# The memory product of an Infini-attention kernel in sixty-four by thirty-two tiles, with a new order of the whole program

## The chip, the cores and the metric

The kernel runs on one core of a Trainium2 chip. The metric is the time of one execution on the device in microseconds; each version is run several times and its median counts. Beside the timed runs there is one profiled execution, whose trace gives start and length of every instruction. TensorE appears in it twice: PE is the matmuls, PEld the loads of their stationary operand ("weights"). DVE is VectorE, ACT is ScalarE, POOL is GpSimd, SP is SyncE, which issues most DMAs.

## The reference

A token sequence of 2048 rows of 512 goes through two branches, which a gate per row mixes. Branch A is attention with 32 heads of 16 in four segments of 512 rows; each segment attends causally within itself and reads a memory that the segments before have built. Branch B is a gated feed-forward net of width 1792. Cut to what matters here:

```
for s in range(4):
    p = softmax(qs @ ks^T * scale + causal mask)
    a_dot = p @ vs                                   # the value products
    pq = phi(qs)
    a_mem = (pq @ M) / (pq @ z + 1e-6)               # the memory is read
    outs.append(g * a_mem + (1 - g) * a_dot)
    pk = phi(ks)
    M = M + pk^T @ vs                                # the memory product
    z = z + sum of pk over the rows
a = concat(outs) @ wo
b = ((x@W_gate) * (x@W_gate > 0) * (x@W_up)) @ W_down
out = gate * a + (1 - gate) * b
```

M holds, for each head, a 16 x 16 matrix; z holds 16 numbers for each head.

## The kernel before, in words

**Layout.** Activations and weights are bf16 and stay in SBUF; sums are made in PSUM, which has eight banks of 128 partitions x 512 float32. Queries and keys are held transposed, in four groups G of 128 rows, a group being eight heads of 16. Values are held by tokens (`vaug`), 17 columns for each head: 16 values and one more that stands for a one, so that the product of weights and values gives the normalizer as its 17th column, and the memory product gives z as its 17th.

**Stages of a segment.** `proj` (line 546) makes q, k and v; `att` (line 650) the scores as 18 "quads" for each segment, into banks 0 to 3 together, one ScalarE exponential for each quad (line 666), the causal masks on GpSimd (line 670), and the value products (`fpv`, line 685, the matmuls in line 694). A half of the value products, for two of the four groups, is two calls of 64 matmuls each. They use 64x32 tiles of TensorE: the contraction is over 64 keys, the row half p picks partitions 0 to 63 or 64 to 127, and each of four column tiles takes the 17 columns of one head; row half 0 sums in one bank, row half 1 in another. Then `nd` (line 619) reads the memory (`num`, line 626, and three VectorE steps in lines 633 to 635), `ffn` (line 740) makes the feed-forward net's hidden layer, `outp` (line 764) its second half and the attention's output, and stores.

**The memory product.** `mu` (line 598) makes it after segments 0, 1 and 2. For each group G and each of four token tiles tt it issues two matmuls in 128x64 tiles (`mode="c"`, line 610): the contraction is over the 128 tokens of the tile, the stationary operand is 64 columns of phi(k), that is four heads, and the moving operand is the same four heads' 68 columns of `vaug`. That makes 4 x 4 x 2 = 32 matmuls, all in one PSUM bank. In each 64 x 68 result only the four diagonal blocks of 16 x 17 are wanted. One VectorE addition, `mum` (line 611), adds the whole 128 x 272 to `Mc`; four GpSimd products (line 615) spread it with a mask to the block diagonal form `Mbd16` that `num` reads, four heads' worth of columns twice.

**What sets the order.** Nothing is ordered by the loops. The program lists all operations with what they read and write, an estimate of how long each holds its engine, and for matmuls the tile mode: f is the full array, r the 32-row tiles of the quads, c the 128x64 tiles, h the 64x32 tiles. `Sched.run` (line 276) then places them in the order written out in the string `ORDER`: two characters stand for a number in base 62, half of it is the operation's number and its parity the engine, where two engines are possible. `BANKS` gives the PSUM bank of each new sum in turn. The order comes from a search outside of the kernel, which uses the same estimates; in `place` (line 220) a change of mode costs it 100 ns (`SWITCH`), and the memory product 520 ns. `place` also puts the waits on semaphores ahead of each operation. Each engine then runs its own list strictly in that order.

Line 705 makes the memory product wait for all that the first value products wait for; line 703 lists it ahead of them.

Of the kernel before, what the change touches and what calls it, by code (L numbers as in the profile page):

```python
# [26 lines left out]
ORDER = (
    "caambOaabQacbSbUaebWbYb8agb0aob2aiaqakcccecgciasckcmcocqcscYaucucwcyeKawfcfOggeMayfefQgicAcCaAcEcGcIcKaCeOcMfgcQcScOfSaEgkeQcUcWfifUbmgmeSbqeUeWeYfkfm"
    "foe1fqfWfYf0f2aGftgogqgsguaIe2f5aKe4gxbifufwe7g4bse8g6aMfagYaOfyg9g0aQf6aSg3hgbof8higygAaUm8gCaWhaaYgbhohcbkhqhsfEhenankfGhua0nwgca2nhnmnyntnogIncfIhI"
    "nqnFfMhKlinugSlkgKbegUfAbufChUa4lcgehWgWnea6legEmQnia8mSlgc0fKnUmVh2gMmeh4lmnWbgmgc2dilYbamKc8n2iegQmiial0ighkmMdclsgGgOlul2hAnImPhmiqlwnKiiishEhMlEnR"  # L30
    "iknMhOl4lAnYbGdglrl6deiClyn0bcl8hwlGb4dknOn4iEdqicoih6hGnSokhQnAbIlIhYmqiyoriOiunCb6lLbMc4omiwnGiQm2iGm4h0bKoolCn6oshSn8lOhCmsiKofdsiWh8oulplQoam6iSiY"
    "owhymumWiAociIoDmYimogi8dam1iUjkiMjajwiojmlSdujyjCmAjgjAjYi0wmjqj0wojcwsi4wqwujsjEoGwxjGkajIoIkcoKjOj2oMjejMwCi2wEi6oOkikeoyj6oQkkkgoAwGjoo4o6oEpskmku"
    "jQpcpEmckwlMoSjKkoo8j4padwoUpemkdypGjukGlUjio1pgkqkIpummpijSpNkCbwpIkylWpKppkAkSpOpkkKkUkEwObAjUoWbyoYjWkOpmkso2k4kMwQk0k6pBw8j8xak2pqkWpwwSkQpyxdkYpY"
    "pCqmk8p0ladAqoqqdCbCqsqaycqcquyeqwyiygykbEqyx6yqsOqCx8sQxAqExoqAxCxqqGybxUdEs0xtxWqIdGs2qKxex0qMx2xYxgdms8c6qOmwtamamoqQqSdomCqUmyxjtkmEqWx5qYxEmItgtm"
    "q0sWq2dIr6q8q4titcdKr8q6twqisaratetyscrssSsYsewAsgrusUsirwdMsktEmGtIsms4rcqetKyup6ymtodQqkywsoyotQtUysqgrytWsMtGreyDtArAsKp2sqtsrgssp8risuxKtut2swdUrk"
    "s6dSt4tYsArCtMsCrmsEp4rEsGtSrGwYuarouetquqtCrIrquguCtOust0rKucuEpQuIwIuGu8rMpSvauKwKySuMyUuOpUrOuWy0rQvgumyWxuuUsyvizsuiyYwMzupWyGy2uwrSuQzAvkyIvmw0yK"
    "yPzkyMw2zgyQvsvozivudWrUwWzQdYzpzSw6zmxnvAvEzqukzwvGuAsIrWwUzywyHyzZvcHAvezCvQvMrYHCvSvwr0vCHsd0HUr2d2Huw4v2xwHIHwv4z2uYHKxyHWz4u0HZuSyydOweAawazUu2HN"
    "yAd4wgIkyEd6ImwczWvqy4xIz0vUy8Ipvyy6xGzauozdzEt6A0zev6IwuuA2zGxMu4IyvIzIt8IAzKvKzMH4uyBcvYzOBowiBed8H6v0BuAev8BsvWAgH9A8DcAmIaBgDeDmDgA4eaIcxlegDowkDi"
    "z6Bir4AiIfvODqAkDsDUz8DWAoAOAQBwAcACAEByAWBqBAAKBCD6AGBID8JgBGAIIYxOAqBKxSEaJiAMBkEeAsEcEgI0AzxQAuAwBMu6I4AAJoEqDSI6I3HQeiISHHJdASAUEsBOIUAYIMekIGIWDQ"
    "IOEuBQECI8EwEEBSJaBEIIJeDuDYCeIQEKEOBaCgDkIKEQEyCiemBUeoBmCkEmE0EABWEGE2BYESB0EoB2D2DwEUCmD0DyE8DAEiB4DCFaD4CoEMDGEIB6DIE4CqDKE6CsDMHOA6B8EkCuDOFkEWFw"  # L40
    "FmCaFcFIEYFyCceqFKIqFOesFACwGeFMCyDEGgFQCSFSHSCAH2ecHEGqCUFUGsCWeuCCCEF2ewGmCGGiGyIsCIIuGACYFWFGCKFsCMF0GoC0FEGKF4C2COGuGMFCC4eyC6JkFgC8NYFeeAGWN0GSJQ"
    "N2GYFiJmN4FoJSGkJqJEFuJGFqJZeCG8GCN8JNG4HaJIGGJKOaGEOcJsGOOeJuGwHkGUJOJwHgHmF6J2JBHcJyG0JUGIJCJ4G6LMF8JWLOKbGQKeG2KgJ0HiJ6HoJ8KmHeLYKcLQMaL0HqGaLSMcLU"
    "MgMeOGL6OEKiL8OIMiKkL2KqMkKoKsMmKCKyKEMsOOKGKKL4KIMuH1OSKOMwOUGcKQKMLgLcMoLeKWLiLlK0O0LmKuO2MyKwMAK2K4KAKSIjMCO4PcOWKUK8MEK6KYPeLoLAMqLsLaLCIgLqIFFYPo"
    "ICN6LILELxPgLuPqO8eeSyOKLyDaLGOMOgSCLKOYSALWPASGPiMGeGPsPCCQPwOiOCOQMIOkPkSEOmPuMKOoPaPMO6MMSIPOPEOsPIMOeIOuPmMQOwPKMSOyPyMUPQPUMWQiPSPWPGQkQoQmQONkQQ"
    "QqQsS8QuTaNmQCQWNoQAP6M0P8M2M4M6TgNEM8Q8NaRaNqS0NcNeQ0NgNsQ2NGQENiSWOqSYS2S5RwMYNuS6RyNwTwNITySKTFRkSMRmNySTNKNMQGQwTARsTcNAQaRIP2TeRKQYSOTiQSSQRgTCRc"
    "NORATGRUQ4NQSURWReNSRoTIQITURCTKRQTMTRP4T6RqUaQKRuUmRSTkPYTmRYT8RMTtToQeUeTONUQgUiQcTSTqNWQ6TWOAP0TuUcRETYROUgUGRGNCT0QUT3UkRiR0UKUrUIUSUPUMUuT4UoUyUs"
    "UUU4UQUwQMUWUDUAU6UER2U1R4R8VdUYVUQyU8U2VgR6VWVYSaV0ScVASeViSkVaVCSmVEV2SoVGSqSgVkVmVeVIeEV4SsVKVoSuWeV6SiVqSwVsVuVMVwVOVyV8VRWgWaWiWkWmWcWoVSWqWsWyWA"
    "WCWEWvWGWIWKWMWwWOWQ"
)
# [284 lines left out]
def program(sc, nc, T, PS, A_x, A_wq, A_wk, A_wv, A_wo, A_beta, W_g, W_u, W_d, gate_w, out, NSEG, KT, NF, NT, EPS, SCALE):  # L334
# [260 lines left out]
    def va(s):  # L595
        return [f"va{s % 2}_{tt}" for tt in range(4)] + ["vone"]

    def mu(s):

        ep = Epoch()  # L600

        def fn(e):
            for G in range(4):
                for tt in range(4):
                    for j in range(2):
                        ins = e.matmul(A(ep)[64 * j:64 * j + 64, 68 * G:68 * G + 68], lhsT=V.phik[:, tt, 128 * G + 64 * j:128 * G + 64 * j + 64],  # L606
                                       rhs=V.vaug[:, s % 2, tt, 8 * G + 4 * j:8 * G + 4 * j + 4, :].rearrange("q h c -> q (h c)"),
                                       start=(tt == 0), stop=(tt == 3), tile_position=(0, 64 * j), skip_group_check=True)
# [2 lines left out]
        d = dve(lambda e: e.tensor_tensor(V.Mc[:], V.Mc[:], A(ep)[:, 0:272].rearrange("q (g c) -> q g c", g=4), ALU.add), t_dve(272), reads=["Mc"], writes=["Mc"], name=f"mum{s}", ep=ep, role="r")
# [294 lines left out]
```

## Time and profile before

| | us |
|---|---|
| median of 3 runs | 263.08 |
| the runs | 262.85 to 263.32 |
| profiled execution | 262.51 |
| its span (first to last instruction) | 261.1 |
| busy in it: PE, PEld, DVE, ACT, POOL | 258.0, 115.8, 186.9, 179.1, 105.9 |
| the memory product's matmuls (L606), 96 | 2.1 busy |
| its addition on DVE (L611), 3 | 0.44 each |
| its products on POOL (L615), 12 | 0.47 each |

The granted TensorE clock is 1.0, full speed. PE's ends are modelled from pipelined starts, so the starts and the chain of waits say more than its busy time. Lines such as L606 are lines of the kernel; "ps<-vaug,phik" names the tile written and the tiles read; "128*64" in a matmul's row is the tile of the array, rows by columns; "x32" is the count. In the timeline the first column is the start, the second the time from the first start to the last end of the group, and brackets tell how long the engine sat idle before it and what ended that. In the chain of waits the columns are start, time, engine, what, and count.

### The profile page before, as it was taken

How to read it: one execution, taken by the hardware profiler on the slowest of the kernel's cores; microseconds unless marked ns; L12 is line 12 of the kernel's file. 1: busy time of each engine (PE TensorE's matmuls, PEld its weight loads, DVE VectorE, ACT ScalarE, POOL GpSimd, SP SyncE). 2: the span in 40 equal slices, each digit the busy share in tenths (PEclk: the TensorE clock that was granted, in tenths of full speed). 3: DMA queues.
4: the chain of work that ended last, by engine and by line, in shares of the span. 5: the costliest groups of instructions: out<-in, count | busy, mean ns of one | idle time of the engine just before them, and what ended most of it. 6: DMA issues, size and time to landing. Idle time of an engine off the chain costs nothing.

```text
span 261.1 us, 6450 instructions
## 1 busy us (share of the span) xinstructions
PE 258.0 (99%) x2665; PEld 115.8 (44%) x2665; DVE 186.9 (72%) x370; ACT 179.1 (69%) x154; POOL 105.9 (41%) x283
## 2 busy tenths in 40 slices
PE   8999999999999999999999999999999999999997
PEld 4644435443544454434544353435344543445444
DVE  1269888698895488888878489778886516568951
ACT  3697988997887897785868687788887765500001
POOL 2010566658106943527511853775057001870000
DMA  6999952018502643220015222002023001020002
GB/s 197 261 247 212 216 86 45 4 41 233 169 25 59 135 99 62 63 62 0 23 29 122 63 60 63 3 0 46 3 55 72 3 20 41 3 60 0 3 3 80
DMA packets 34684, 19.34 MB, mean 74 GB/s; under 512 B 24032, under 2 KB 34144, under 8 KB 34656
## 3 DMA queue, kind: packets, MB, share of 16 engines
q1 hardware_dynamic: 34272, 18.67, 29.6%
q8 instruction: 21, 0.34, 0.5%
q10 hardware_dynamic: 384, 0.27, 0.3%
q14 instruction: 7, 0.06, 0.1%
HBM read 9.87 MB, written 2.11 MB: 46 GB/s over the span
## 4 chain that ended last, share of the span: by engine, by line
PE 97%; DMA 1%; ACT 1%; ACTq 0%; DVE 0%; issue 0%
PE ps L750 38%; PE ps L789 19%; PE ps L563 10%; PE ps L662 9%; PE ps L694 7%; PE ps L782 6%; PE ps L561 5%; DMA hT<-in_A_x_dram 1%; PE ps L626 1%; PE ps L554 1%; PE ps L606 1%; ACT L381 0%; PE ps L461 0%; ACTq L368 0%; DVE osb L798 0%; ACT rden L381 0%
## 5 line engine op out<-in xcount | busy, mean ns | idle before, releaser
L666 ACT ACTIVATE E<-ps 128x2048 bf16<-128x2048 f32 x72 | 135.1, 1877 | 38.0 <-PE ps L662 37.6
L670 POOL TENSOR_SCALAR_AFFINE_SELECT E<-E 128x256 bf16<-128x256 bf16 (+1 forms) x256 | 98.3, 414 | 123.2 <-ACT E L666 61.4
L750 PE MATMUL ps<-xT,wu 128*128 128x512 bf16 x224 | 60.8, 380 | 0.0
L750 PE MATMUL ps<-xT,wg 128*128 128x512 bf16 x224 | 60.0, 380 | 0.0
L789 PE MATMUL ps<-wd,hT 128*128 128x512 bf16 (+2 forms) x238 | 55.9, 367 | 0.0
L761 DVE TENSOR_TENSOR hT<-ps,rl 128x512 bf16<-128x512 f32 x56 | 38.2, 685 | 14.8 <-PE ps L750 13.1
L750 PEld LDWEIGHTS ps<-xT,wg 128*128 128x128 bf16 x224 | 20.7, 98 | 26.5 <-issue 2.4
L759 DVE TENSOR_SCALAR rl<-ps 128x512 bf16<-128x512 f32 x35 | 23.9, 686 | 11.0 <-PE ps L750 10.7
L750 PEld LDWEIGHTS ps<-xT,wu 128*128 128x128 bf16 x224 | 20.4, 98 | 25.7 <-issue 3.2
L789 PEld LDWEIGHTS ps<-wd,hT 128*128 128x128 bf16 x238 | 21.2, 98 | 24.0 <-issue 3.7
L662 PE MATMUL ps<-qT,kp 32*128 32x128 bf16 (+7 forms) x512 | 28.6, 287 | 0.0
L708 DVE STREAM_TRANSPOSE Tn<-ps 128x512 f32<-128x512 f32 x32 | 21.2, 696 | 3.8 <-PE ps L694 3.4
L798 DVE TENSOR_SCALAR osb<-ps,omg 128x512 bf16<-128x512 f32 (+1 forms) x15 | 10.6, 718 | 16.9 <-PE ps L789 9.9
L662 PEld LDWEIGHTS ps<-qT,kp 32*128 32x128 bf16 x512 | 8.2, 92 | 27.7 <-ACT E L666 12.3
L799 ACT ACTIVATE osb<-ps,omg 128x512 bf16<-128x512 f32 (+1 forms) x2 | 1.3, 634 | 26.8 <-PE ps L782 26.8
L563 PE MATMUL ps<-xT,wk 128*128 128x512 bf16 x64 | 17.9, 380 | 0.0
L694 PE MATMUL ps<-E,vaug 64*17 64x128 bf16 (+7 forms) x512 | 17.8, 283 | 0.0
L694 PE MATMUL ps<-E,vsh 64*17 64x128 bf16 (+7 forms) x512 | 17.6, 283 | 0.0
L561 PE MATMUL ps<-wv,xT 128*128 128x512 bf16 x64 | 17.3, 380 | 0.0
L758 ACT ACTIVATE rl<-ps 128x512 bf16<-128x512 f32 x21 | 12.4, 595 | 6.0 <-PE ps L750 4.6
L782 PE MATMUL ps<-wo,oT 128*128 128x512 bf16 (+2 forms) x68 | 16.3, 367 | 0.0
L694 PEld LDWEIGHTS ps<-E,vaug 64*17 64x17 bf16 x512 | 12.2, 86 | 3.6 <-issue 0.8
(71 smaller groups left out, 226.8 us busy)
## 6 DMA issues: line engine op xcount, KB each, us to landing
vsh<-vaug SPq DMA_DIRECT2D x8, 272.0 KB, 3.3
out_dram<-osb SPq DMA_DIRECT2D x15, 128.0 KB, 1.8
wg<-in_B_W_gate_dram SPq DMA_DIRECT2D x8, 224.0 KB, 3.2
wu<-in_B_W_up_dram SPq DMA_DIRECT2D x8, 224.0 KB, 4.0
osb<-in_A_x_dram SPq DMA_DIRECT2D x12, 128.0 KB, 2.0
wd<-in_B_W_down_dram SPq DMA_DIRECT2D x3, 512.0 KB, 6.4
wq<-in_A_wq_dram SPq DMA_DIRECT2D x4, 128.0 KB, 3.0
wk<-in_A_wk_dram SPq DMA_DIRECT2D x4, 128.0 KB, 3.3
```

The costliest lines, as they stand in the source:

```text
L561: ins = e.matmul(A(ep)[:, :], lhsT=V.xT[:, kt, s % NX, col * 128:(col + 1) * 128], rhs=w[:, kt, :], start=(kt == 0), stop=(kt == KT - 1))
L563: ins = e.matmul(A(ep)[:, :], lhsT=w[:, kt, col * 128:(col + 1) * 128], rhs=V.xT[:, kt, s % NX, :], start=(kt == 0), stop=(kt == KT - 1))
L662: ins = q.matmul(PS[:, jj, o:o + 512 - 64 * c], lhsT=V.kp[r, kslot(s, G), c, :], rhs=V.qT[r, qslot(s, G), 64 * c:512], start=True, stop=Tr ...
L666: acts.append(act(lambda a: a.activation(V.E[:, e, :, :], PS[:, 0:4, :], ACT.Exp, scale=SCALE), t_act(2048), writes=[f"E{e}"], name=f"exp{ ...
L670: pools.append(pool(lambda g, ap=ap, base=base: g.affine_select(out=ap, in_=ap, compare_op=ALU.is_ge, fill=0.0, base=base, pattern=[[0, 4] ...
L694: ins = q.matmul(A(eps[2 * g + p])[32 * jj:32 * jj + 17, 64 * c:512], lhsT=v[:, 8 * G + 2 * jj + p, :], rhs=V.E[r, e, jj, o:o + 512 - 64 * c],
L708: ds.append(dve(lambda e, p=p, ep=eps[2 * (G - G0) + p]: e.transpose(V.Tn[:, p, :], A(ep)[:, :]), 706, writes=[f"Tn{p}"], name=f"tr{s}_{G} ...
L750: ins = e.matmul(A(ep)[:, :], lhsT=w[:, kt, f * 128:(f + 1) * 128], rhs=V.xT[:, kt, c % NX, :], start=(kt == 0), stop=(kt == KT - 1))
L759: ("dve", lambda e, ep=eg, r=r: e.tensor_scalar(V.rl[:, r, :], A(ep)[:, :], 0.0, None, ALU.max), t_dve(512))],
L761: evs.append(dve(lambda e, ep=eu, r=r, hs=hs: e.tensor_tensor(V.hT[:, hs, :], A(ep)[:, :], V.rl[:, r, :], ALU.mult), t_dve(512), reads=[f" ...
L782: ins = e.matmul(A(ep)[:, 0:c1 - c0], lhsT=V.oT[:, o0 + G, i * 128:(i + 1) * 128], rhs=V.wo[:, G, c0:c1], start=st_ and G == 0, stop=sp_ a ...
L789: ins = e.matmul(A(ep)[:, 0:c1 - c0], lhsT=V.hT[:, slots[f], i * 128:(i + 1) * 128], rhs=V.wd[:, f, c0:c1], start=st_ and f == f0, stop=sp ...
```

## The change

The memory product is issued in the 64x32 tiles of the value products. For each group G and token tile tt there are eight matmuls: row half p (64 of the 128 tokens) by column tile j (32 columns of phi(k), two heads), with the two heads' 34 columns of `vaug` moving. That makes 4 x 4 x 2 x 4 = 128 matmuls. Row half 0 sums in one bank, row half 1 in another. `Mc` keeps 34 columns for each group where it kept 68; two VectorE additions of 128 x 136 add the two banks to it, one after the other. The four GpSimd products spread it to `Mbd16` as before, two heads' columns four times. The estimate for the product is 430 ns in mode h.

The estimate for the transposed loads of x (`load_x`) becomes 190,000 bytes and 1200 ns of SyncE where it was 131,072 and 1350, and the order and the banks are searched anew with these numbers. An unused constant goes. The diff without the strings:

```
-        ("Mc", [128, 4, 68], F32), ("Mbd16", [128, 4, 136], BF16), ("mumask", [128, 4, 136], F32),
+        ("Mc", [128, 4, 34], F32), ("Mbd16", [128, 4, 136], BF16), ("mumask", [128, 4, 136], F32),
...
-                           1 << 17, occ=1350.0, writes=[f"xT{c % NX}_{kt}"] + ([] if c % NX else [f"xT0_{kt}{h}" for h in range(2)]), name=f"ldx{c}_{kt}"))
+                           190000, occ=1200.0, writes=[f"xT{c % NX}_{kt}"] + ([] if c % NX else [f"xT0_{kt}{h}" for h in range(2)]), name=f"ldx{c}_{kt}"))
...
     def mu(s):
 
-        ep = Epoch()
+        eps = [Epoch(), Epoch()]
+        eps[0].group = eps[1].group = (eps[0], eps[1])
 
         def fn(e):
             for G in range(4):
                 for tt in range(4):
-                    for j in range(2):
-                        ins = e.matmul(A(ep)[64 * j:64 * j + 64, 68 * G:68 * G + 68], lhsT=V.phik[:, tt, 128 * G + 64 * j:128 * G + 64 * j + 64],
-                                       rhs=V.vaug[:, s % 2, tt, 8 * G + 4 * j:8 * G + 4 * j + 4, :].rearrange("q h c -> q (h c)"),
-                                       start=(tt == 0), stop=(tt == 3), tile_position=(0, 64 * j), skip_group_check=True)
+                    for p in range(2):
+                        r = slice(64 * p, 64 * p + 64)
+                        for j in range(4):
+                            ins = e.matmul(A(eps[p])[32 * j:32 * j + 32, 34 * G:34 * G + 34], lhsT=V.phik[r, tt, 128 * G + 32 * j:128 * G + 32 * j + 32],
+                                           rhs=V.vaug[r, s % 2, tt, 8 * G + 2 * j:8 * G + 2 * j + 2, :].rearrange("q h c -> q (h c)"),
+                                           start=(tt == 0), stop=(tt == 3), tile_position=(64 * p, 32 * j), skip_group_check=True)
             return ins
-        m = pe(fn, 520.0, reads=[f"phik{g}" for g in range(4)] + va(s), name=f"mu{s}", ep=ep, role="w", mode="c")
-        d = dve(lambda e: e.tensor_tensor(V.Mc[:], V.Mc[:], A(ep)[:, 0:272].rearrange("q (g c) -> q g c", g=4), ALU.add), t_dve(272), reads=["Mc"], writes=["Mc"], name=f"mum{s}", ep=ep, role="r")
+        m = pe(fn, 430.0, reads=[f"phik{g}" for g in range(4)] + va(s), writes=[eps[1].res], name=f"mu{s}", ep=eps[0], role="w", mode="h")
+        d = [dve(lambda e, p=p: e.tensor_tensor(V.Mc[:], V.Mc[:], A(eps[p])[:, 0:136].rearrange("q (g c) -> q g c", g=4), ALU.add), t_dve(136), reads=["Mc"], writes=["Mc"], name=f"mum{s}_{p}", ep=eps[p], role="r") for p in range(2)]
...
-            j2 = lambda t, G=G: t[:, G, :].rearrange("q (j c) -> q j c", c=68)
-            ps.append(pool(lambda e, G=G, j2=j2: e.tensor_tensor(j2(V.Mbd16), V.Mc[:, G, :].unsqueeze(1).to_broadcast([128, 2, 68]), j2(V.mumask), ALU.mult), t_pool(136, 2.2),
+            j4 = lambda t, G=G: t[:, G, :].rearrange("q (j c) -> q j c", c=34)
+            ps.append(pool(lambda e, G=G, j4=j4: e.tensor_tensor(j4(V.Mbd16), V.Mc[:, G, :].unsqueeze(1).to_broadcast([128, 4, 34]), j4(V.mumask), ALU.mult), t_pool(136, 2.2),
...
-                put(dmu=[mem[1]], poolmu=mem[2])
+                put(dmu=mem[1], poolmu=mem[2])
```

The strings `ORDER` and `BANKS` are replaced as a whole. In the new order the set of operations is the old one with three more additions. The three memory products stand where they stood, between a quad and the first value products. At the start, TensorE has the query products and the transposes of the first input more mixed, the two filler matmuls first, all four k products ahead of the first quad, and v behind it; in the middle the feed-forward and output products are distributed anew among the quads; the last value products come seven TensorE groups earlier. The choice between VectorE and ScalarE changes for some fifty PSUM copies and the like.

More of the change, by code (lines that the diff above doesn't have):

```diff
@@ L17 @@
 LAT = 60.0
-MU_G = 1
 PE_LAT = 175.0
@@ L27 @@
 ORDER = (
[L28 to L47, printed above, removed]
@@ L48 @@
-    "WCWEWvWGWIWKWMWwWOWQ"
+    "bYbObQcYamaaacaeagaoaqaicaciakauccckayascscecmcucqcgcocwggeKfObScyaweMfccAfeaYfQaKcEcGcCcKcScIgicQcMcOfSgkeOfgfifkfmaCeQeSbqaAcUfobUeUeWaEcWgmfqeYe0fs"
+    "gogqc0fUfWfYaGf0bWb4f2b6f5gsaIgue2e4bee6f6f8b0fufwgbbsb8e8fagwgygAhggcc2c8hagefzfAgDhcfGhegGgYg0hifCgSgUhsg2g4g6g8fEnanmhuc4aOaMbkncgWbininohInynvnAbo"
+    "bmmSlemUhwhKhAhCfIlggKhUgEaQmWaWlilklmgIhWaUc6nKhyhQhohSlulwh2nHaShknenglzmYa0lon8m0baoah4iagMdciem3ignMiiiknkmMnCimmOnEhYh0iqnTlGfMlIbuhmmRdihMhOdemg"
@@ new lines @@
+    "nIhqisiymiiAlLmsmudgbgmkdkiCiEiKgOiGl0l2ocoemwlAnqiOl4ohm4nsnOoim6hEnwlClEnWm8nYicl6lPioiQnQiun4nUiWa6a8lSoogQmml8man0dmoklqoma4a2owiYfKlQotn2oqn6ouoy"
+    "h6h8dqi8hGjkjmiIoEjojybIjEdoiSiUiwiMjAjCb2lsjabMbGjgj0dajwbKwqjcwsj2wujibcwwwywBwGjGdsjIjKj4kckej8jQwIoIoKjOjeo6o8kgj6wLoRkkkaoMoAoOoCjupii4kmkojMkqkw"
+    "oSjsmCpkkioGpfpakypckAoUduoWo2kskuprpukIdwdykCkEkKkQjSjUjWkSpGpglUpIkMkOjYpKpMi6pOpwpQmokUoYjqo0o4xci0i2kWk2bApDxexhkYwSk6pmlMpok8dApypsk0wUpAkGwXp0qo"
+    "lak4pEdClcqqmyp2p8qabCquqcqeygqsyiqwqylYykbyymyoyasQyuycdEqAqExsxubwx4x6sSsUxxs2s4yexExGqGxYx0xiqIx3taqCqKqMqObEsWxkqQqSqUqkqmtctetitkp4mftmtoqWqYtus6"
@@ new lines @@
+    "x9s8lWdGsOmAmcq0mqmEq2mGxIxmdImKq4dKdQtyq6r8sap6q8tAwDrarurwscsetKtMsgsisktwryrArCtOsmsorEqgqitSyytWyAyHyqysywtYt0rGrItgt4mIssrcsuswsysYrergsMrirLsCrk"
+    "sEsGsqsIrmt6rowMt2tQtqugrrs0usuuuwuGtGtstItCtEuitUuIuouKuMt8uOdSuQvcvew0uSuYdUyCyEvguauUrOrQyIdWvorsu0pUrSrUrWyOvqwOwQucyKvwxoyMrYr0xyyTvywEyWvkviuyu2"
+    "u4yYy4yQyUvIy8zczedYd0zazhy0uEzivKvUuew2vWy2y6vMr2u6zwzUr5ukumzyzFzWv6sKzAv8wazkw4sAu8w6vazmvYzozqzszCzuxOvEwipWuAvGpYvQvAvOxKxNzGvmwZpSH0H2v0z3zIzKHE"
+    "HyvSHAwkzRzMHGwezOH5A4d2d4uWIqHJA6vCHCz6Isuqz8xAvszSvuIvBsuCAexCBgAaxQxSdMAiBwBiIaIcIfAcd6AkAqDqByDgv2v4d8zYz0eaAgIgIiwgICxWrMIEDixrIlAmAoDkDsDmDuDwBc"
@@ new lines @@
+    "xUIHDYAGAIz4ASAUwmwoAswcBuBABCBEBKxaD0AOEaAKA0HOHQBoISBGBMBOBQDWr6DUAMEcEiD2D4IUHTIWAWAYEkEqecBSEmAuA2AwA8BaAQEuI4EeI6egAyADEwIMAAEGI9JaJeIOdOEIw8IRBq"
+    "AEJcekJgESEUBUEWBWEYBIEOEQD6D8JiEgBYCiB0emB2E0E4E6eiE8BeB4B6B8CaCcJkDKDMEsDAHUDyIYI0DCI3CkCmCoCqDOEyIwDQDEFcFeDoBkDGECEKEMEEeoJmCeeqCsCuCwCyJoJuFoeeEo"
+    "BmFAesFOE2FCFEFaEADIFUFIFGFqFsFuFQGkCCFMFSeuCWHWCEGmGsDSFWFYF0F6F2F8GwCGGyCICYCKC0GAGEGCGGGMGIFkHKCMCOFKeweyHYeAC2C4CQGoGQGSCAC6GUFwFyHMC8GYG0DaDdFmJq"
+    "IoIyCgCSIAGWGaGcN4G2GOG4HaN6DeJsJKJMN8OaJWJYGeJwJSHeHcJ5OeOgOiJyJOJQOkHgHiJAHqJ8JUFgKaJCJEJ0H8FiJHJIHkGKHsHuLSJ2J6KkLUKmKsHmHoHwKcKeL4KhKiGqGuMgL6GgMk"
@@ new lines @@
+    "G6G8MiMmMoOKOMKoOOKqKwKyKuKEMqMsMuKIKKL8OYOUOWKQMaMyKAMcMeKCKUO0O2H6MAKYK0KWOIO6KGInK3LiLkKMKOeCO8PaLuLwPiPkeEK4KSL0LaLcLCF4K6PeMCLrLmK8L2PmPuLfLoMwLg"
+    "LyS2LsLALGLILWPwMEPyPALEMGMIPCPECUPGLKPgLOSESGLMLYSQSSGiMKPIPqOcS4PSPKLQMMSNMOMQSZTbILIJPMO4MSeGeIPsPoMUMWOQOSPUPWPYMYM0P0M2PcQoQuPOPQQqP2P4P6M4QUP8M6"
+    "M8NaNcQWQYQaQsQcNeQwQeNgNiQyQAQIQ2SINkQkQmReRgNKQ4SKSONMNmRiNORmRoRkQGQ6Q8NoNqNsTeNuRCNQNSTgRaQgNwRERGRKNyQ0RqRsRuRyTnRAOoNARwRINUNWNYOqNCOsOuROS6QKQM"
+    "QCQOS8TcN1RQSUSWTiS0R0TCTETkTLUYToU0R2UcOyOAOCQQOmOEOGUgOwTGTITMTONENGRMTQRWUeUlTSUiTUTqUmTsUsUoUqTXTYUxTzTuUuUyUMTwTAUORST4T0UQRUUST2T6UVRYU7QiRcT9Ua"
@@ L49 @@
+    "R8SeR4R6SaScQESgSiSkSqVGVmNIVoVqVsU2U4UEUAUCSsUWVIWkV0WmU8VaV2SuWoWqSmSwVeSySAV4V6VuSCUGVgVcVKVMN2SoV8WsUJUKVjVkVwVyQSVAVCVEVOVQVSVUVWVYWaWcWeWgWuWwWy"
+    "WiWEWGWIWKWMWOWAWCWQWSWUWW"
 )
 BANKS = (
-    "450674654756475765745645767654764674564765657467564465466754675454675674674544454657641757457547546754674567456134675764574656746574755645675456475476"
-    "5476456754546754675645746744457654674664465452604131675031742365310265"
+    "326454654754674656756456546574654764756476565745645675475464756747457464654667667465476546767467456564765764576024756746574645647564715354675465745764"
@@ L53 @@
+    "7645657467546464754647567456454657647455567562035701234012560230146237547"
 )
```

## Prediction

> **What bounds the kernel now.** I read the page first, its parts 1 and 4, then the chain of waits in order of time, then the timeline around the first memory product.
>
> ```profile
> span 261.1 us, 6450 instructions
> ...
> PE 258.0 (99%) x2665; PEld 115.8 (44%) x2665; DVE 186.9 (72%) x370; ACT 179.1 (69%) x154; POOL 105.9 (41%) x283
> ...
> PE 97%; DMA 1%; ACT 1%; ACTq 0%; DVE 0%; issue 0%
> ```
>
> The chain that ended last is TensorE for 97% of the span. Busy PE time is partly modelled, but the chain says the same: TensorE waits for almost nothing, so a microsecond more or less of its own work is a microsecond of the kernel, and a change on the other engines counts only where it makes TensorE wait. The chain around the first product:
>
> ```profile
> 43.23 0.43 PE ps L561 x2
> 43.99 0.63 PE ps L606 x28
> 44.62 2.14 PE ps L694 x127
> 47.09 1.83 PE ps L563 x8
> ```
>
> The product (L606) holds TensorE 0.63 us, directly ahead of the value products (L694), which take 2.14 us for 128 matmuls. The chain has the product two more times, also at 0.63 us (at 93.56 and 153.44). All three lie fully on the path: together 1.89 us. The timeline says what fills one of them:
>
> ```profile
> 43.92 0.58 PEld L606 LDWEIGHTS ps<-vaug,phik 128*64 128x64 bf16 x32 [0.21 <-issue]
> 43.92 0.70 PE L606 MATMUL ps<-vaug,phik 128*64 128x68 bf16 x32
> 44.55 0.09 PEld L694 LDWEIGHTS ps<-E,vaug 64*17 64x17 bf16 x4
> 44.56 0.11 PEld L694 LDWEIGHTS ps<-E,vsh 64*17 64x17 bf16 x8
> 44.59 0.09 PEld L694 LDWEIGHTS ps<-E,vaug 64*17 64x17 bf16 x4
> ...
> L606 PE MATMUL ps<-vaug,phik x96: 192/195/219, 43.9 to 153.9; 128*64 128x68 bf16 x96
> ```
>
> The 32 matmuls start over 0.70 - 0.195 = 0.505 us, some 16 ns apiece (two column tiles side by side, 68 columns each). The value products' first weights come at 44.55, 0.63 us after the product's first, so 0.125 us lies between the last matmul's start and them. A stream of 68 columns takes about 0.03 us of it (512 columns take 0.215 us, from the chain's 1.83 us for 8 at L563); the other 0.095 us is TensorE changing from 128x64 tiles to 64x32 ones.
>
> **The change, part by part.** *The switch.* The product now uses the value products' tiles, and the new order, read by the rule of lines 278 to 281, still places each product between a score quad and the value products. The change of tiles ahead of it stays; the one behind it goes: -0.095 us each. Counting tile changes along both orders gives 151 and 148, so nothing else changes here.
>
> *The matmuls.* 32 pairs of weight load and matmul become 128 of 34 columns in eight tiles. Streamed, 16 rounds of 34 columns would take 16 x 0.015 = 0.24 us, less than now. But the number of pairs grows fourfold, and the question is how fast TensorE is given them. The trace shows two rates, on the same eight or four weight loads of the value products:
>
> ```profile
> 45.60 0.14 PEld L694 LDWEIGHTS ps<-E,vsh 64*17 64x17 bf16 x8
> 45.66 0.11 PEld L694 LDWEIGHTS ps<-E,vaug 64*17 64x17 bf16 x4
> ...
> 241.00 0.16 PEld L694 LDWEIGHTS ps<-E,vsh 64*17 64x17 bf16 x8
> ...
> L694 PEld LDWEIGHTS ps<-E,vsh x512: 82/88/88, 44.6 to 241.9; 64*17 64x17 bf16 x171
> ```
>
> At 44.56 eight loads take 0.11 us; one lasts 0.083, so they start (0.11 - 0.083)/7 = 4 ns apart: these were issued ahead, while TensorE changed tiles. At 45.60, in the second half of the same products, nothing was waiting, and the same eight take 0.14 us, 8 ns apart; the four at 45.66 take 0.11 us, 9 ns apart; at 241.00 it is 11 ns. They lie in different tiles and overlap, so it is not the loads' length that spaces them but the arrival of new pairs: about 8 ns a pair once what was issued ahead is used up. Sixteen pairs at the fast rate are seen at 44.55 to 44.59. So one product takes 16 x 4 + 112 x 8 = 0.96 us, plus 0.015 us of stream: 0.98 us, against 0.63: **+0.35 us each, +1.05 us for three**. Bounds: 128 pairs all at 4 ns give 0.51 us (-0.12 each); all at 11 ns 1.41 us (+0.78 each). I take 8 because 112 of 128 pairs come after the first sixteen, in the situation of the 45.60 rows. The value products behind start with no pairs issued ahead; the second half starts so already and takes no longer than the first (128 in 2.14), so nothing for that.
>
> *The sums.* One 272-wide add on VectorE becomes two 136-wide ones.
>
> ```profile
> L611 DVE TENSOR_TENSOR Mc<-Mc,ps x3: 436/437/439, 44.7 to 154.1; 128x272 f32<-128x272 f32 x3
> ...
> 91.54 0.19 DVE L633 TENSOR_TENSOR rdm<-ps,epsv 128x32 f32<-128x32 f32 x1 [0.62 <-PE ps L626]
> 91.76 0.35 DVE L634 RECIPROCAL rdm<-rdm 128x32 f32<-128x32 f32 x1
> 92.15 0.75 DVE L635 SCALAR_TENSOR_TENSOR amem<-ps,gexp,rdm 128x512 bf16<-128x512 f32 x1
> 92.82 1.40 DVE L798 TENSOR_SCALAR osb<-ps,omg 128x512 bf16<-128x512 f32 x2
> 94.23 0.44 DVE L611 TENSOR_TENSOR Mc<-Mc,ps 128x272 f32<-128x272 f32 x1
> 95.40 1.31 DVE L708 STREAM_TRANSPOSE Tn<-ps 128x512 f32<-128x512 f32 x2 [0.73 <-PE ps L694]
> ...
> 91.08 0.42 PE L626 MATMUL ps<-Mbd,phiq 128*128 128x136 bf16 x4
> 93.48 0.70 PE L606 MATMUL ps<-vaug,phik 128*64 128x68 bf16 x32
> ```
>
> Each of the two lies between the 32-wide add (0.19) and the 272-wide (0.44); at 0.3 the pair takes 0.6, 0.17 us more. Behind it VectorE waits 0.73 us for the value products anyway, so it costs nothing; without that cover, 0.17 us each. The adds wait for a product that ends 0.35 us later; queued behind them are the transposes of the value products, which end later too. GpSimd's four 136-wide products stay. The second bank: the second product takes one that the last memory read (L626) releases through L633 to L635. Now the product starts 93.48 - 91.08 = 2.40 us after the read, with four output groups between; the new order leaves three, 0.43 less: 1.97. The three steps end at 92.90, 1.82 after the read's start. The margin of 0.15 us is thin, but it is one: nothing.
>
> *The start.*
>
> ```profile
> 3.90 0.45 PE L476 MATMUL ps<-const-bfloat16-1.0 128*128 128x256 bf16 x2
> ...
> 4.30 0.61 PE L554 MATMUL ps<-xT,wq 128*128 128x256 bf16 x4
> 5.09 0.61 PE L554 MATMUL ps<-xT,wq 128*128 128x256 bf16 x4 [0.18 <-DMA wq<-in_A_wq_dram]
> 6.08 0.28 PE L461 MATMUL ps<-ident,hT 128*128 128x128 bf16 x2 [0.15 <-DMA hT<-in_A_x_dram]
> ...
> 6.69 2.40 PE ps L554 x22
> ```
>
> TensorE waits for the second wq tile until 5.09, having done four query matmuls; the new order places three ahead of the first that needs it, so one (2.40/22 = 0.11 us) moves behind the wait: **+0.1 us**. The two filler matmuls (0.45) move to the front, where the inputs are awaited anyway.
>
> *The loads.* The transposed loads are charged 45% more bytes, and the new order starts the feed-forward products later and gets several loads in another sequence. On SyncE the small beta load is moved ahead of the wv loads, and ScalarE's exponential of it ahead of the third query copy. By
>
> ```profile
> 3.61 1.86 SPq L368 DMA_DIRECT2D wk<-in_A_wk_dram  x4
> ...
> braw<-in_A_beta_dram SPq DMA_DIRECT2D x1, 8.0 KB, 3.7
> ```
>
> it is issued at about 5.5 and lands at 9.2, when that copy's matmuls end (6.69 + 2.40 = 9.09): 0.1 us of waiting for a bank that is not needed at once, nothing. The loads' own waits on TensorE now are 0.18 + 0.15 us, so retiming can win 0.3 us at most. Elsewhere the new order moves 480 of 601 TensorE groups, and tells no price: from -0.3 (those waits gone) to +0.75, a bank that comes free one VectorE step late (the L635 row). I take 0.
>
> **Sum.** 1.05 + 0.1 = +1.15 us. The profiled run took 262.51 us, 1.4 more than its span, which makes 263.66 there; the median of the runs, 263.08, lies 0.57 us (0.2%) higher, so **264.2 us**. A difference of 0.2%, 0.53 us, is about what this measurement can tell from none.
>
> **The rivals.** *The pairs keep up* (faster): all 128 pairs at the 4 ns of the 44.56 row, or bound by each tile instead. The point that decides is 0.63/128 = 4.9 ns a pair. For it: nothing in the trace has more than some sixteen pairs ready, so a long run of short ones has not been seen. Against: the 45.60 rows. At 4 ns: 3 x -0.12 + 0.1 = -0.26; where the stream of 0.24 us sets it, without the switch, 3 x (0.24 - 0.63) + 0.1 = -1.07; the middle, -0.67, gives 262.4. [...]
>
> *Instructions run out.*
>
> ```profile
> q8 instruction: 21, 0.34, 0.5%
> ```
>
> 21 packets for 5,330 TensorE instructions: about 254 each; 0.5% of 16 x 261.1 us / 21 is 1.0 us a packet. A product is now 256 instructions in 0.98 us, where 256 took 2.14 before. If only one packet is held ahead, TensorE starves by up to the packet's 1.0 us in each product; +0.7 each on top: 264.2 + 2.1 = 266.3. Against: the value products at 2.14 us never starved.
>
> *The order misses.* Bank and exponential waits that the planner misjudges; one thin spot is the second product's bank. Two VectorE steps of 0.75 in TensorE's way are +1.5: 265.7. Against: the order before, made by the same planner, left hardly a wait.
>
> *A floor for each matmul.* If the 16 ns between the starts of L606 were not the two tiles' stream but what every small matmul costs, 128 would take 2.05 us, +1.42 each: 267.4. The 4 ns of the value products speak against it. [...]
>
> **How the numbers follow.** Forecast 0.55 (its own range 263.6 to 265.2), pairs keep up 0.22, instructions run out 0.12, order misses 0.09, floor 0.02. The range 262.2 to 266.4 takes in the pair rate's bounds (11 ns gives 263.08 + 2.34 + 0.1 = 265.5) and the order's; it leaves out the fastest part of the second case (0.07), half of the third and the floor, 0.15. Faster by over 0.53 us: half of the second case, 0.11. Within: the other half and 0.03 of the forecast, 0.14. Slower: the rest, 0.75.
>
> **What would show it.** Right: L606 with 384 matmuls, some 0.98 us from its first weight load to the value products' first, no gap ahead of these, weight loads 8 ns apart in its later part; PE still 97% of the chain, the start near 9.2. Wrong: L606 at 0.5 us or less; or holes inside it beside an instruction packet; or TensorE idle on VectorE or ScalarE elsewhere by more than some tenths.

## The result and the profile after

The changed kernel takes 271.81 us (six runs, 271.49 to 273.46) against 263.20 for the kernel before, measured beside it (six runs, 262.85 to 263.49). The ratio is 1.0343, with a 95% interval of 1.0325 to 1.0362: 8.6 us slower. The forecast was 264.2 with a range up to 266.4. The profiled execution took 272.8 us, its span 271.5.

The page of the kernel after, its parts 1, 3 and 4:

```profile
span 271.5 us, 7018 instructions
...
PE 261.0 (96%) x2953; PEld 118.2 (44%) x2953; DVE 188.1 (69%) x369; ACT 182.0 (67%) x158; POOL 113.9 (42%) x283
...
q8 instruction: 23, 0.38, 0.6%
...
PE 91%; issue 3%; DVE 2%; DMA 1%; ACT 1%; POOL 0%; SPq 0%
```

TensorE is still the chain, but for 91% of it where it was 97%, and 3% is now "issue": time in which TensorE was waiting for nothing that the profile shows. TensorE's waits, grouped by line, with total, count and the longest in us:

```profile
PE ps L696 <- issue: 4.5, 3, 2.1
PE ps L664 <- issue: 2.5, 2, 1.4
...
PE ps L553 <- DMA wq<-in_A_wq_dram: 0.7, 1, 0.7
```

Five waits make 7.0 us. None is at the product (L608): three lie within the value products (L696), two ahead of score quads (L664). The timeline of TensorE at the first of them:

```profile
44.35 1.19 PE L608 MATMUL ps<-vaug,phik 64*32 64x34 bf16 x128
45.44 0.39 PE L696 MATMUL ps<-E,vaug 64*17 64x512 bf16 x4
...
46.35 0.24 PE L696 MATMUL ps<-E,vsh 64*17 64x128 bf16 x8
46.41 0.44 PE L696 MATMUL ps<-E,vaug 64*17 64x64 bf16 x5
48.25 0.39 PE L696 MATMUL ps<-E,vaug 64*17 64x512 bf16 x3 [1.41 <-issue]
```

The product takes 1.1 us, the first call of the value products goes as it should, and one matmul into the second call, whose wait the weight load ahead of that matmul had passed, TensorE stops for 1.41 us. What moved on the DMA queues meanwhile (packets, MB, share), from 45.8 to 46.9 us:

```profile
DMA packets 1, 0.02 MB, mean 15 GB/s; under 512 B 0, under 2 KB 0, under 8 KB 0
q8 instruction: 1, 0.02, 5.7%
```

and from 46.9 to 48.3 nothing at all. One instruction packet, 1.0 us long (5.7% of 16 x 1.1 us), ends at 46.88 by its record; TensorE goes on at 48.25. The packets before the other four holes end at 97.12, 101.02, 162.32 and 188.24, and TensorE goes on at 98.56, 102.47, 163.82 and 189.61: each time 1.4 to 1.5 us after a packet's end. Counting TensorE's instructions in the trace in their order (weight loads, matmuls and the few semaphore instructions between them), the first after each hole is number 960, 2240, 2496, 3776 and 4544. Each is a multiple of 256 plus 192. So instructions come in blocks of 256, the five holes stand at the borders of blocks, and TensorE had spent the block that it held before the next one was there.

The time that a block lasts decides. Before, the shortest ran 3.54 us (4288 to 4544, from 201.8 us) and there was no hole. After, the blocks that end at the five holes were spent, from the start of their first instruction to that of their last, in 1.63, 1.03, 2.24, 1.70 and 2.14 us. At three of these holes the packet of the next block starts 1.0 to 1.2 us after TensorE has entered the block that it holds (at the second 0.2 us before, at the fourth 1.7 after), takes 0.9 to 1.3, and its instructions start some 1.4 later: 3.4 to 3.9 us in all (2.4 and 4.1 at those two). Each of the five blocks was spent sooner than that, and TensorE was left with nothing. A product and the value products behind it are now 256 + 256 instructions in 3.2 us, and wherever the borders fall, one block lies wholly within them.

The traces of all twelve kernels bear this out, and narrow it. In none does the first instruction of a block start sooner than 1.2 us after its packet's end, and behind each of their 28 holes TensorE goes on 1.2 to 1.6 us after it. Of the 31 blocks spent in under 2.8 us, 27 end in a hole; at the other four the next packet had started 1.0 to 2.5 us before the block's first instruction ran. So what counts is when the packet lands, and the 3.5 us of theory A below hold where it starts about 1.1 us after the border.

### The profile page after: what moved, and what is told of

Its sections match the earlier page's. It is cut to its first block, busy times and chain, and to the rows that moved or that the text cites. A ratio compares the mean times of both kernels' runs of the same rounds, so it can differ in the third digit from the quotient of the medians.

```text
span 271.5 us, 7018 instructions
## 1 busy us (share of the span) xinstructions
PE 261.0 (96%) x2953; PEld 118.2 (44%) x2953; DVE 188.1 (69%) x369; ACT 182.0 (67%) x158; POOL 113.9 (42%) x283
## 4 chain that ended last, share of the span: by engine, by line
PE 91%; issue 3%; DVE 2%; DMA 1%; ACT 1%; POOL 0%; SPq 0%
PE ps L752 35%; PE ps L791 18%; PE ps L664 9%; PE ps L562 8%; PE ps L696 7%; PE ps L560 5%; PE ps L784 5%; PE ps L628 1%; PE ps L608 1%; DMA wq<-in_A_wq_dram 1%; PE ps L553 1%; ACT E L668 1%; POOL E L672 0%; DVE hT L763 0%; SPq L367 0%
## 5 line engine op out<-in xcount | busy, mean ns | idle before, releaser
L672 POOL TENSOR_SCALAR_AFFINE_SELECT E<-E 64x256 bf16<-64x256 bf16 (+1 forms) x256 | 106.0, 438 | 117.8 <-ACT E L668 56.4
L752 PE MATMUL ps<-xT,wu 128*128 128x512 bf16 x224 | 59.6, 380 | 0.0
L791 PE MATMUL ps<-wd,hT 128*128 128x512 bf16 (+2 forms) x238 | 54.9, 367 | 0.0
L791 PEld LDWEIGHTS ps<-wd,hT 128*128 128x128 bf16 x238 | 21.9, 98 | 24.9 <-issue 1.7
L664 PE MATMUL ps<-qT,kp 32*128 32x128 bf16 (+7 forms) x512 | 29.0, 287 | 2.5 <-issue 2.5
L664 PEld LDWEIGHTS ps<-qT,kp 32*128 32x128 bf16 x512 | 8.4, 92 | 30.3 <-ACT E L668 14.8
L696 PE MATMUL ps<-E,vsh 64*17 64x64 bf16 (+7 forms) x512 | 18.3, 283 | 3.1 <-issue 3.1
L696 PE MATMUL ps<-E,vaug 64*17 64x384 bf16 (+7 forms) x512 | 18.6, 283 | 1.6 <-issue 1.4
L562 PE MATMUL ps<-xT,wk 128*128 128x512 bf16 x64 | 16.5, 380 | 0.0
L800 DVE TENSOR_SCALAR osb<-ps,omg 128x512 bf16<-128x512 f32 (+2 forms) x12 | 8.4, 703 | 10.9 <-PE ps L791 6.0
L696 PEld LDWEIGHTS ps<-E,vaug 64*17 64x17 bf16 x512 | 12.5, 86 | 5.5 <-issue 2.5
L760 ACT ACTIVATE rl<-ps 128x512 bf16<-128x512 f32 x20 | 11.8, 596 | 3.6 <-PE ps L752 3.5
L696 PEld LDWEIGHTS ps<-E,vsh 64*17 64x17 bf16 x512 | 11.2, 87 | 5.0 <-issue 3.7
```

Of the source, the lines that this page charges most:

```text
L562: ins = e.matmul(A(ep)[:, :], lhsT=w[:, kt, col * 128:(col + 1) * 128], rhs=V.xT[:, kt, s % NX, :], start=(kt == 0), stop=(kt == KT - 1))
L664: ins = q.matmul(PS[:, jj, o:o + 512 - 64 * c], lhsT=V.kp[r, kslot(s, G), c, :], rhs=V.qT[r, qslot(s, G), 64 * c:512], start=True, stop=Tr ...
L672: pools.append(pool(lambda g, ap=ap, base=base: g.affine_select(out=ap, in_=ap, compare_op=ALU.is_ge, fill=0.0, base=base, pattern=[[0, 4] ...
L696: ins = q.matmul(A(eps[2 * g + p])[32 * jj:32 * jj + 17, 64 * c:512], lhsT=v[:, 8 * G + 2 * jj + p, :], rhs=V.E[r, e, jj, o:o + 512 - 64 * c],
L752: ins = e.matmul(A(ep)[:, :], lhsT=w[:, kt, f * 128:(f + 1) * 128], rhs=V.xT[:, kt, c % NX, :], start=(kt == 0), stop=(kt == KT - 1))
L791: ins = e.matmul(A(ep)[:, 0:c1 - c0], lhsT=V.hT[:, slots[f], i * 128:(i + 1) * 128], rhs=V.wd[:, f, c0:c1], start=st_ and f == f0, stop=sp ...
```

## The experiments

Theory A is the one above: TensorE runs out of instructions. Against it stood at first the new order (B in the first four expectations), and then the product itself, its pairs, switches, tiles or second bank, costing the time where it stands (the rivals of the later ones, each as its expectation says). All ten runs, with the idle time of TensorE in the holes at the borders of blocks. Idle time counts from the modelled end of the last matmul and so understates a hole; from the last start ahead of a hole to the first behind it, the five holes of after come to 8.8 us in place of 7.0:

| run | median, us | ratio to before, 95% | idle in holes, us |
|---|---|---|---|
| after, shifted by 180 instructions | 271.67 | 1.0354 [1.0308, 1.0401] | 1.0, 2.0, 1.8 |
| before, shifted by 124 | 266.15 | 1.0122 [1.0097, 1.0147] | 0.6, 1.2, 1.0 |
| new order, old product | 262.95 | 0.9996 [0.9975, 1.0017] | none |
| old order, new product | 274.26 | 1.0437 [1.0411, 1.0463] | five, 6.1 in all |
| after, 8 fillers behind each product | 272.84 | 1.0359 [1.0324, 1.0394] | 0.9, 0.9 |
| after, 24 fillers | 280.52 | 1.0647 [1.0617, 1.0678] | none |
| after, half of the product | 270.08 | 1.0244 [1.0208, 1.0280] | 0.8, 2.4, 1.0, 1.0 |
| after, shifted by 96 | 270.20 | 1.0266 [1.0229, 1.0303] | 1.0, 0.4, 1.8, 1.5 |
| new order, old product, 24 fillers | 282.88 | 1.0736 [1.0676, 1.0796] | 2.0 |
| half of the product, 24 fillers | 279.58 | 1.0616 [1.0559, 1.0673] | 0.9 |

**The two halves of the change.** In the first kernel the order is the new one and `mu` is the old text, in the second the order is the old one and `mu` the new text. Cut from the first, against after:

```
-        eps = [Epoch(), Epoch()]
+        ep = Epoch()
...
-                    for p in range(2):
+                    for j in range(2):
...
# ORDER and BANKS: those of after, without the three added additions and the second banks
```

> The new order with the old memory product (32 matmuls in 128x64 tiles, one bank, one addition). Theory A: counted along the trace no block is done too soon, so no hole; the start's 0.4 us stays: 263.3 to 264.0. Theory B: the order's waits stay, 268 to 270. Theory C: 263.2 to 263.6.

> The old order with the new memory product (128 matmuls in 64x32 tiles, two banks, two additions behind each other); for the second bank a few sums change banks, no operation changes its place. Theory A: the product's own time adds 1.3 us, and five holes come up at about the places of the changed kernel (46, 95, 97, 156, 180 us), 7.5 to 8.7 us: 271.5 to 273. Theory B: 264.5, the product's own time alone. Theory C: as slow as the changed kernel less the order's share, 268 to 272, but with the time inside the product and not in holes behind it.

The order alone ran as before, without even the 0.1 to 0.8 us that A had left for the start, so it is out. The product alone loses 11.0 us, more than the whole change and 1.3 more than A's upper end. TensorE's waits in its profile:

```profile
PE ps L697 <- issue: 4.4, 3, 2.0
PE ps L665 <- issue: 1.8, 2, 1.2
```

Five holes again, at 49.3, 99.9, 103.6, 164.7 and 192.0 us; the last stands some 30 us behind the third product. From start to start they come to 8.1 us, which with 1.3 us for the products leaves some 1.6 of the 11.0. Beside them TensorE is idle 0.25 us at 11.6 (a load of wv), 0.6 at 21.4 and 0.4 at 45.6 and 178.0 us, which it isn't in the kernel before. The profiled run, the longest of four (275.36), ran at a mean granted clock of 0.994, of which more below.

**The same matmuls, the blocks shifted.** Some of the five matmuls of `warm` at the start give way to small ones whose only use is their number; the rest of the program is what it was, but 180 (after) or 124 (before) places further on:

```
-        for i in range(5):
+        for i in range(92):                      # before: 63
+            p, j = i % 2, i // 2 % 4
+            e.matmul(PS[32 * j:32 * j + 32, 3 - p, 0:34], lhsT=ones[64 * p:64 * p + 64, 0:32], rhs=wide[64 * p:64 * p + 64, 0:34], tile_position=(64 * p, 32 * j))
+        for i in range(3):                       # before: 4
             ins = e.matmul(A(epw), lhsT=ones, rhs=wide)
```

> The kernel before with its TensorE instructions moved by 124: one of the five filler matmuls at the start is replaced by 63 tiny ones with their weight loads. Neither the memory product nor the order is altered. Theory A: where the kernel before had no hole, four appear, of about 0.9 to 1.3 us, in the value products near 46, 97, 156 and 242 us; 3.5 to 4.2 us more, 266.7 to 267.5. Theories B and C: 263.2, as before.

> The changed kernel with its TensorE instructions moved by 180: two of the five filler matmuls at the start, which run while the first input is awaited, are replaced by 92 tiny 64x32 ones with their weight loads. Nothing behind them is altered. Theory A, instructions run out: TensorE's instructions come in blocks of 256, one block is held ahead, the next is asked for when a block is begun and can be run some 3.5 us later; a block that is done sooner makes TensorE wait. Counted along the trace of the changed kernel, the five holes then become three: about 1.4 us in the value products behind the first memory product, 2.0 behind the second, 1.7 behind the third, and none in those near 186; 5.2 us instead of 7.8, so 268.5 to 269.5 us. Theory B, the new order makes TensorE wait for other engines: 271.8, holes where they were. Theory C, the 128 small matmuls themselves are slow: 271.8.

The old kernel shifted, with the old product and the old order, gets what it never had. Its waits, and TensorE's timeline in the middle of the first value products:

```profile
PE ps L698 <- issue: 1.6, 2, 1.0
PE ps L786 <- DVE rdg L718: 1.2, 1, 1.2
...
47.31 0.40 PE L698 MATMUL ps<-E,vaug 64*17 64x320 bf16 x8
48.30 0.28 PE L698 MATMUL ps<-E,vsh 64*17 64x256 bf16 x8 [0.59 <-issue]
```

+2.9 us, with 2.8 us idle in three holes, a little under A's 266.7 to 267.5; the fourth that A counted, near 242, did not come: its block was spent in 2.0 us, but the packet had started 1.0 us before it. The profiled run (266.8) also waits 0.9 us for a load of wv at 12.2. One of the three holes is put down to VectorE (rdg); but TensorE stops between two weight loads of one product, whose wait the first had passed at 98.56 us, a packet ends at 98.29, and the second load starts at 99.65, 1.4 us later, as behind the others. In the kernel before, the same product starts ahead of that VectorE step. The shift does it with nothing of the change in the kernel, so the new product isn't needed for a hole.

The new kernel shifted had its holes at the three places counted and none at 186, 4.7 us in place of 7.0, and its profiled run took 269.99. But its median did not fall: by the number alone it is B's and C's 271.8, and only the places of the holes speak for A. What may have stood in the way shows in the runs' mean granted TensorE clock: the run at 1.000 took 269.99, two at 0.994 took 272.30 and 271.04, one at 0.987 took 273.57. The next run shows where the clock goes.

**Another shift.**

```
+        for i in range(48):
+            e.matmul(PS[...], lhsT=ones[...], rhs=wide[...], tile_position=(64 * p, 32 * j))
         for i in range(5):
```

> The changed kernel with 48 matmuls of 64x32 tiles on constants ahead of the five that warm TensorE, which are all kept: 96 instructions more at the start, 0.4 us of work. Theory A: the boundaries of 256 instructions fall 96 instructions earlier in the program; counted holes 2.1 at 46, 1.65 at 97, 1.3 at 158 us, 5.1 in all in place of 8.5, none at 181 us: 271.8 - 3.4 + 0.4 = 268.8 us, 267.5 to 270. Rivals B and C: 271.8 to 272.3 us. If the holes lie where A has them and the time doesn't fall, what the run of the kernel with 92 such matmuls showed is repeated: runs differ in how long the packets take, and the median needs more than the count.

271.98 in the profiled run, 269.01 to 271.43 in the others; the median, 270.20, lies just above A's 267.5 to 270 and below the rivals' 271.8. The holes stand at 47.4, 101.0 and 165.5, as counted, and there is a small one at 72.7 that was not. Behind the hole of 1.8 us idle at 101 the stretches of TensorE read (us, busy, then the clock granted and the DMA share and GB/s):

```profile
101.00:102.00 1.00, 1.00 (x51) 0.68 (x51) 0.64 (x2) 0.00 (x0) 0.00 (x0) 0.96 0.00 0
102.00:105.00 3.00, 3.00 (x12) 1.04 (x9) 1.21 (x2) 1.88 (x1) 0.78 (x2) 0.50 0.02 5
105.00:106.00 1.00, 1.00 (x8) 0.32 (x6) 0.00 (x0) 0.00 (x0) 0.00 (x0) 0.84 0.00 0
```

Half clock for 0.08 + 3.0 + 0.32 = 3.4 us, which costs half of it, 1.7 us: four matmuls of 128x512 take 1.89 us in it (at 102.0 us), where four in the kernel after take 1.04 at full clock (at 49.7). So a long hole has a second price, in some executions: in the profile of after, a hole of 2.1 us idle left the clock at 1.00, here one of 1.8 did not. Why holes of the same length cost this only sometimes no run shows. The first shift fits it: 269.99 without a spell of half clock, one spell (0.006 of 270 us is 1.6 us) in two of its runs, two in one, though only the mean clock of those runs is on record. In place of the 268.5 to 269.5 expected, 269.99 is still half a microsecond more. And spells are not all: the five other runs of this kernel, all at full clock, differ by 2.4 us among themselves.

**Work that thins the block.** Eight, then 24, matmuls of 128x512 on constants between each product and its value products:

```
                 G = G0 + g
+                for i in range(8 if g == 0 and mem else 0):      # the other run: 24
+                    q.matmul(A(eps[0]), lhsT=const[128, 128], rhs=const[128, 512], start=True, stop=True)
                 for c in range(8):
```

> The changed kernel with eight matmuls of 128x128x512 on constants put between each product and its value products, into a bank that the value products then overwrite: 16 instructions and about 1.9 us more work at each of three places, +5.75 us in all by 0.216 us each and 0.19 us for two switches. Theory A (TensorE starves where a block of 256 of its instructions is spent in under about 3.5 us): the fillers stretch the dense block, so the five holes shrink from 8.5 us by my count to 3.5 (near the second product 2.1, at the third 0.4 and 1.0, none at the first, none by the 181 us value products): 271.8 + 5.75 - 4.9 = 272.7 us, 271.5 to 274. Rival B (the lost time belongs to the product's pairs, their switches or the operands' waits): the work adds to it, 277.5 us. A hole of over 1 us at the first product speaks against A.

> As the run with eight, with 24 matmuls on constants at each of the three places: +16.1 us of work. Theory A: holes left 0.4 us by my count, so 271.8 + 16.1 - 8.0 = 279.9 us, 278.5 to 281. Rival B: 287.9 us. Work on other engines could hide nothing of this, as TensorE is the one on the chain throughout.

5.75 us of work added 1.0 us, 16.1 us of it 8.7: A's 272.7 and 279.9 against 272.84 and 280.52, the rival's 277.5 and 287.9 far off. TensorE's waits with eight, then those of the run with 24, which has no hole left:

```profile
PE ps L664 <- issue: 0.9, 1, 0.9
PE ps L608 <- issue: 0.9, 1, 0.9
```

```profile
PE ps L475 <- PEq L895: 0.8, 1, 0.8
PE ps L698 <- POOL E L672: 0.2, 1, 0.2
```

The eight left a hole of 0.9 us idle within the second product and one of 0.9 at 166.6, where 2.1, 0.4 and 1.0 were counted. With 24 the timeline has the product and its fillers back to back:

```profile
43.88 1.19 PE L608 MATMUL ps<-vaug,phik 64*32 64x34 bf16 x128
45.00 5.42 PE L690 MATMUL ps<-const-bfloat16-1.0 128*128 128x512 bf16 x24
50.35 0.39 PE L698 MATMUL ps<-E,vaug 64*17 64x512 bf16 x4
```

The fillers hold TensorE from 45.00 to 50.35, 5.35 us, and three times that is 16.05: 280.52 - 16.05 = 264.5 us is what the changed kernel takes without holes, and the other 7.3 of the 271.8 are holes.

**Half of the product.**

```
-                for tt in range(4):
+                for tt in range(2):
...
-                                           start=(tt == 0), stop=(tt == 3), ...
+                                           start=(tt == 0), stop=(tt == 1), ...
```

> The changed kernel with the product over two of each segment's four groups of 128 tokens: 64 matmuls in place of 128; half of the memory sum is left out. At 8.3 ns a pair each product takes 0.55 us in place of 1.06. Theory A: the time falls by 3 x 0.53 = 1.6 us of pairs and the counted holes fall from 8.5 to 5.2 (1.3 at 47, 1.1 at 68, 1.2 at 97, 1.5 at 156 us; none at 181): 271.8 - 5.0 = 266.8 us, 266 to 268. Rival B (each lost microsecond belongs to the products' own pairs, so half of the pairs lose half): 267.5 us, with holes at the products alone. Rival C (the lost time hangs on there being two banks, two additions or tiles, whatever the number of pairs): 271.8 - 1.6 = 270.2 us. The place of a hole tells A from B: one near 68 us, where no product runs, and none at 181 us.

270.08: neither A's 266.8 nor B's 267.5, and it looks like C's 270.2. The places speak for A: the value products at 71.3, near which no product runs, have the longest hole, and there is none near 189. Its sizes were wrong. TensorE's waits:

```profile
PE ps L696 <- issue: 3.5, 2, 2.4
PE ps L664 <- issue: 1.8, 2, 1.0
```

2.4 us at 71.3 in place of 1.1, and a spell of half clock behind it (0.994 in that run). The packet that this hole waited for started 2.4 us behind its border, not 1.1. On the DMA queues from 66.5 to 69 us, ahead of it:

```profile
q1 hardware_dynamic: 1016, 0.68, 167.1%
q8 instruction: 1, 0.02, 2.4%
```

the engines were loaded beyond their time (167%) with weights for the output and the second feed-forward product. That the packet queued behind those is the likeliest reading; it was not tried.

**What the fillers and half of the product cost by themselves.** The fillers in the kernel with the new order and the old product, and behind the half product:

> The changed kernel's order with the old product of 32 matmuls, and the 24 matmuls on constants between product and value products, as in the run with 24 of them: what those cost by themselves where no hole was. The order alone ran at 262.95 us, the work added counts 16.1 us: 279.1 us. Theory A: the new product with the same 24 ran at 280.5 us, and without holes it should cost three times 0.43 to 0.5 us more than the old one, so 279.0 to 279.2 us here. Rival: if the 24 matmuls cost more than they count (a switch, a wait behind them), this run lies near 280.5 and the new product without holes costs nothing.

> The product over half of the tokens (64 matmuls, half of the memory sum left out) with the 24 matmuls on constants behind it. Theory A: no hole is left, so the pairs alone tell it from the run of 128 matmuls with 24: 3 x 64 x 8.33 ns = 1.6 us less than 280.5, 278.9 us. It then lies no more than 0.3 us from the old product with 24. If the half product's 270.1 us without the 24 matmuls was not holes and their spells of half clock, but something of its own, this run shows it as well: about 280.8 us, since 266.8 was counted there.

The first missed by 3.7 us, on neither side's number. The 48 instructions more ahead of it had moved a border. Its waits, and its timeline at the hole:

```profile
PE ps L661 <- issue: 2.0, 1, 2.0
...
71.68 0.39 PE L695 MATMUL ps<-E,vaug 64*17 64x512 bf16 x4
...
73.82 0.39 PE L661 MATMUL ps<-qT,kp 32*128 32x384 bf16 x7
76.19 0.23 PE L661 MATMUL ps<-qT,kp 32*128 32x128 bf16 x1 [1.98 <-issue]
```

A block from 71.7 to 74.0 us held 256 instructions of value products and quads, with no product and no filler within 20 us. So a pair of value products starves TensorE just as well when the borders fall around it. Its packet (73.78 to 74.74) started 2.1 us behind the border; it, too, met the weight loads. The one run at full clock took 281.42, less 2.0 idle 279.4, beside the 279.0 to 279.2 expected; the other three were at 0.994 and took 1.4 to 2.6 more. The half product with fillers took 279.58, of which 0.9 is a hole at 196.1: 278.7, beside 278.9, where a cost of its own, as in C, would have given 280.8. Without holes, then, the old product, the half and the whole new one stand at 279.4, 278.7 and 280.5: the whole new product costs about 1.1 us, and 192 pairs make 1.8. That the half lies 0.7 under the old, not within 0.3 of it, and that the old with the fillers taken off (279.4 - 16.05 = 263.4) lies 0.4 over its own 262.95, show that such figures hold to some half a microsecond.

No run points to a kernel that beats both: the new order is worth nothing measurable, and the new product costs about 1 us where no hole is.

## Why the prediction was wrong, point by point

**The pairs: right, a little low.** "About 8 ns a pair" was 8.33: groups of eight start every 66.7 ns. The row of the first product's weight loads:

```profile
44.35 1.09 PEld L608 LDWEIGHTS ps<-vaug,phik 64*32 64x32 bf16 x128 [0.21 <-issue]
```

(1.09 - 0.09)/127 is 7.9 ns, with a fast start of the first thirty, some 3.4 ns apiece, where the first sixteen at 4 ns were supposed. From the first weight load to the value products' first the three products took 1.06, 1.01 and 1.19 us where 0.98 was said: +0.43, +0.38 and +0.56, in sum +1.4 for +1.05. The third has a pause of 0.13 us inside. The value products' first weight load comes 0.06, 0.01 and 0.06 us behind the product's last, where it was 0.15 before: the change of tiles between them is gone, as said.

**The sums: right.**

```profile
L613 DVE TENSOR_TENSOR Mc<-Mc,ps x6: 295/296/297, 45.6 to 161.6; 128x136 f32<-128x136 f32 x6
```

0.296 us each for the 0.3 taken, and nobody on TensorE waited. The second bank held: the second product took 1.01 us and starts 0.33 us behind its quad like the other two; the step that frees the bank ends 0.15 us ahead of it, the margin that was said.

**The start: right in sign, short in size.** The second wq tile came 0.66 us late for TensorE, where 0.18 was before:

```profile
5.75 0.38 PE L553 MATMUL ps<-xT,wq 128*128 128x256 bf16 x2 [0.66 <-DMA wq<-in_A_wq_dram]
```

The query matmuls ended 0.43 us later in this execution, not 0.1. In the runs of the order alone nothing of it is left in the median.

**The order: right.** Nothing was said, and the order alone ran at 0.9996 of before.

**The step that failed**: the forecast's sum has no term for instructions that arrive too late. They stand only in the rival "instructions run out", which got 0.12 and 2.1 us and was the case, at 7.3. Its condition, "if only one packet is held ahead", fits the traces: the 42 packets of before and after whose blocks ran started from 2.0 us ahead of the first instruction of the block before their own to 3.4 us behind it. And the page of the profile gave its size, 254 instructions a packet. What failed is the sentence that set it aside: "the value products at 2.14 us never starved". They are 256 instructions, as many as a block; they could starve only where the borders fall around them, and before they fell otherwise: the shortest block ran 3.54 us, and the packet for the block behind it had ended 2.2 us before that block's first instruction, where 1.2 to 1.6 are the least. That was luck of the count: 124 instructions more at the start made it 2.9 us slower. The trace had what was needed: the instructions can be counted and each block timed, and the packets' records stand beside them. And it was priced at 0.7 us a product, with the packet's own 1.0 us as the most, when its start, some 1.1 us after the border, and the 1.4 us from its end to the first instruction count as well: waits of 1.0 to 2.1 us, and not in the products themselves but in whatever stood behind them, and at 189.6 us behind value products with no product near, where the 192 instructions more of each product had moved a border to.

The terms of the result, from the medians: without holes +1.3 (264.5 to 263.2; forecast +1.15), holes +7.3.

## What to carry to other kernels

Count TensorE's instructions, not only its time, and time each block of 256, from the borders that the instruction packets and the holes show. In these twelve traces 27 of the 31 blocks spent in under 2.8 us ended in a hole; at the other four the next packet had started 1.0 to 2.5 us before the block's first instruction ran, and a block of 3.54 us had no hole. In the kernel after, a packet that started 1.0 to 1.2 us behind the border gave instructions 3.4 to 3.9 us behind it; in the two runs where one started 2.1 and 2.4 us behind, the holes were 2.0 and 2.4 us idle. Cutting the product into small tiles made 128 matmuls of 32, and beside the 256 instructions of the value products a whole block then fitted into the dense stretch; and an edit that adds or removes instructions shifts every border behind it, so compare the shortest blocks before and after. A difference of a few us that follows an edit elsewhere in the program may be just such a shift: 124 instructions more at the start made the kernel before 2.9 us slower.
